# The router's noise in one tile, multiplied in PSUM, and its ranks summed in PSUM, in a retention and mixture-of-experts kernel

## The chip, the core and the metric

The kernel runs on one core of a Trainium2 chip. A core has five engines that run at the same time, each with its own queue of instructions, executed in order: TensorE (PE in the profile; its weight loads are PEld), VectorE (DVE), ScalarE (ACT), GpSimd (POOL) and SyncE (SP), which here only issues DMAs. GpSimd and ScalarE can issue DMAs too. SBUF is the large on-chip memory of 128 partitions; PSUM is the smaller one that TensorE writes its results to, and that VectorE and ScalarE can read and write. The metric is the device time of one execution in microseconds. A profile is one separately profiled execution; its span runs from the first to the last instruction.

## What is computed

Two layers run one after the other. The first is a retention layer, attention without a softmax, in which each score is multiplied by a power of a decay that depends on the head:

```python
scores = scale * np.matmul(q, k.transpose(0, 1, 3, 2))          # 8 batches, 8 heads, 576 tokens, 64 wide
gamma = 1.0 - 2.0 ** (-5.0 - np.arange(H, dtype=np.float32))
Dmat = np.where(rel >= 0, gamma[:, None, None] ** rel[None, :, :], 0.0)
attn = np.matmul(scores * Dmat[None], v)
```

Its output, 4608 tokens of 512 numbers, goes through a mixture of 8 experts. A router picks two experts for each token:

```python
logits = x @ w_gate
noise_scale = np.log1p(np.exp(x @ w_noise))
noisy_logits = logits + noise_scale * noise          # noise: 4608 x 8, an input
top2 = np.argpartition(-noisy_logits, 2, axis=1)[:, :2]
top2_w = softmax over the two chosen values
out[token] = sum over its two experts e of  top2_w * (relu(x[token] @ w1[e]) @ w2[e])
```

## The kernel before, in words

**Order.** The engines' order is the order in which the program is written: the whole of attention and routing, and then the expert stage, stand under a manual schedule, so no scheduler moves anything. A tile framework adds the waits between engines.

**Attention.** Sixteen units (four pairs of batches, two groups of four heads, two batches of the pair) go through a software pipeline, one unit a step `n`. For a unit, SyncE loads q, k and v four units ahead (lines 170 and 175; the last 64 tokens of each batch, the tail, at 182). GpSimd multiplies k and q by the decay and casts them to bf16 (`cast_k`, line 203, and `cast_q`, line 212), ScalarE casts v (189). TensorE transposes (253), forms the scores (268), which VectorE masks into SBUF (273), then the states (292) and the outputs (318 and 326). Tails have their own scores (343, masked at 345) and outputs (356 and 359). The input tiles hold four units at a time.

**Routing.** When the four units of a pair of batches and its tail are done, `route(bp)` starts; it is a generator, and the main loop runs one of its pieces between the parts of each later step (`piece()`), so that its instructions stand in the queues among those of attention. It runs four times. A pair has 1152 tokens, held as 9 columns of 128: columns 0 to 3 and 4 to 7 are four tokens a partition of the first and the second batch, column 8 holds the two tails, 64 partitions each. One PSUM bank, `R`, is kept for the router: it takes the logits (line 518), the ranks (614 to 622), the sums of the columns (columns 200 to 215 of the bank), the lists of tokens (288 to 367), and holds two constants (368 to 376, and from 384 on).

In a route, VectorE adds the two halves of the logits into `lg` (525 and 526); ScalarE computes log(1 + exp) of the noise half (529 and 530) into the SBUF tile `nl`; VectorE multiplies by the noise, eight columns from `noise` and the ninth from `noiset` (553 and 554), and adds the gate's logits (555). Two searches for the largest value follow (`first_max`, lines 545 to 550), and a one-hot matrix `M` of the two choices (572). From `M`, TensorE counts how many earlier tokens chose each expert (614 to 622), in PSUM as `pr`. VectorE adds the counts of earlier pairs (`base`, line 627, into the SBUF tile `prf`), adds the two choices of each token (629, into `prs`), multiplies both by `M` (630 and 631, into the third and fourth part of `pd`), and sums over experts (633). It then brings `base` up to date (636; in two routes 638 too), copies a transposed row of tokens out of PSUM (512) and works out positions (643 to 663). GpSimd computes what the rows carry beside the token (584 to 608, 635, 652 to 656), and SyncE stores them (658). Two comparisons make one-hot matrices (670 to 677), from which TensorE makes the lists of tokens of each expert (687).

**What is queued around it.** GpSimd's casts for a later unit stand in its queue behind its routing instructions, SyncE's later loads behind the route's stores. The noise is loaded once, in step 1, by SyncE (`load_noise`, lines 480 and 484), behind the gate's weights (1191 and 1192) and ahead of unit 6's q, k and v.

**Experts.** Five tiles of 256 tokens run early, among the last steps of attention (`early`, lines 365 to 440); the other 35 follow, each with a gather by GpSimd (848), transposes (957), two matmuls (973 and 993), and the sum of a token's two experts (1034, scattered at 1040).

Of the kernel before, what the change touches and what calls it, by code (L numbers as in the profile page):

```python
# [10 lines left out]
F32 = mybir.dt.float32  # L11
BF16 = mybir.dt.bfloat16
I32 = mybir.dt.int32
AX = mybir.AxisListType.X
Alu = mybir.AluOpType
Act = mybir.ActivationFunctionType

P = 128
N = 4608
NCOL = N // P  # L20
E = 8
# [23 lines left out]
HD = 64  # L45
MID = 288
NC9 = 9
# [85 lines left out]
class Attention:  # L133
# [3 lines left out]
    def __init__(self, tc, ctx, raw, K, q, k, v):  # L137
        self.tc, self.nc, self.K = tc, tc.nc, K
        self.src = dict(q=q, k=k, v=v)
        nc = self.nc  # L140
        ep = lambda n, b, **kw: ctx.enter_context(tc.tile_pool(name=n, bufs=b, **kw))
        self.cp = ep("at_c", 1)
        self.raw = raw
        self.bf = ep("at_bf", 2)
        self.tp = ep("at_t", 2)
        self.sp = ep("at_s", 2)
        self.xp = ep("at_x", 2)
        self.ps = ep("at_ps", 1, space=bass.MemoryType.PSUM)
        self.Tb = [self.cp.tile([P, 2, 4, P], BF16, name=f"Tb{j}") for j in range(4)]
        self.u = {}  # L150
        self.tails = {}
        self.T = {}
        self.xT = {}
# [289 lines left out]
class Router:  # L443
    def __init__(self, tc, ctx, K, at, wgn, moe_noise, xd, keep):
        self.tc, self.nc, self.K, self.at = tc, tc.nc, K, at
        self.wgn, self.xd, self.keep = wgn, xd, keep
        nc = self.nc
        self.sp = ctx.enter_context(tc.tile_pool(name="rt", bufs=2))
        self.one = ctx.enter_context(tc.tile_pool(name="rt1", bufs=1))
        self.rows = ctx.enter_context(tc.tile_pool(name="rtx", bufs=3))  # L450
        self.noise = self.one.tile([P, 8, 4, E], F32, name="noise")
        self.noiset = self.one.tile([P, 4, E], F32, name="noiset")
        self.L = self.one.tile([P, NH], F32, name="L")
        self.moe_noise = moe_noise
        self.w = self.one.tile([P, 2, NCOL], F32, name="w_all")
        self.ov = self.one.tile([P, 2, NCOL], F32, name="ov_all")

        bank = self.bank = at.ps.tile([P, 512], F32, name="R", bufs=1)
        self.iota = bank[:, 384:]
        self.local = bank[:, 368:368 + NC9]  # L460

        self.base = self.one.tile([P, 2, E], F32, name="base")
        self.atleast = {}
# [13 lines left out]

    def load_noise(self, q):
        nm = self.moe_noise.rearrange("(b s) e -> b s e", b=8)
        q.dma_start(out=self.noise.rearrange("p b r e -> p b (r e)"),  # L480
                    in_=nm[:, :512, :].rearrange("b (p r) e -> p b (r e)", r=4))
        nt = nm[:, 512:, :].rearrange("(p b) s e -> s b p e", b=2)
        for j in range(2):
            q.dma_start(out=self.noiset[j * HD:(j + 1) * HD], in_=nt[:, j])

    def route(self, bp):

        nc, K, sp = self.nc, self.K, self.sp
        V = nc.vector
        ps = self.at.ps  # L490
        C = NC9
# [32 lines left out]
        lg = sp.tile([P, C, 2 * E], F32, name="lg")  # L524
# [2 lines left out]
        yield  # L527
        nl = sp.tile([P, C, E], F32, name="nl")
        nc.scalar.activation(nl, lg[:, :, E:], Act.Exp)
        nc.scalar.activation(nl, nl, Act.Ln, bias=1.0)  # L530
        yield
        row(2)
        yield
# [1 line left out]
        def col(name):  # L535
            return sp.tile([P, C], F32, name=name)
# [13 lines left out]
            V.tensor_reduce(w, s, AX, Alu.max)  # L550
            return m, w

        V.tensor_mul(nl[:, :8], nl[:, :8], self.noise[:, 2 * bp:2 * bp + 2].rearrange("p b c e -> p (b c) e"))
        V.tensor_mul(nl[:, 8], nl[:, 8], self.noiset[:, bp])
        V.tensor_add(nl, nl, lg[:, :, :E])
        yield
        m1, w1 = first_max(nl, "a")
        yield
# [11 lines left out]
        SH = [P, C, 2, E]  # L570
        M = sp.tile(SH, BF16, name="M")
# [10 lines left out]
        pd = sp.tile([P, 4] + SH[1:], F32, name="pd", bufs=1)  # L582
# [8 lines left out]
        r = col("r")  # L591
# [20 lines left out]
        pr = self.bank[:, :C * 2 * E].rearrange("p (c a e) -> p c a e", c=C, a=2)  # L612
# [10 lines left out]
                             stop=(c == C - 1), skip_group_check=True)  # L623
        yield

        prf = sp.tile(SH, F32, name="prf", bufs=1)
        V.tensor_tensor(prf, pr, self.base.unsqueeze(1).to_broadcast(SH), Alu.add)
        prs = sp.tile([P, C, E], F32, name="prs", bufs=1)
        V.tensor_tensor(prs, prf[:, :, 0], prf[:, :, 1], Alu.add)
        V.tensor_mul(pd[:, 2], M, prf)  # L630
        V.tensor_tensor(pd[:, 3], M, prs.unsqueeze(2).to_broadcast(SH), Alu.mult)
        yield
        V.tensor_reduce(red, pd, AX, Alu.add)
# [657 lines left out]
```

## Time and profile before

| | |
|---|---|
| median of 7 runs | 526.05 us (522.96 to 534.98) |
| the profiled execution | 526.33 us |
| its span | 524.3 us |
| its mean granted TensorE clock | 0.92 |
| busy PE, DVE, ACT, POOL | 426.5, 239.2, 275.3, 277.0 us |
| TensorE in 90 to 120 us | 23.5 of 30 us busy, granted clock 0.74 |
| TensorE in 210 to 300 us | 86.0 of 90 us busy, granted clock 1.00 |
| routes, from L525 to the last L677 | 56, 97, 135 and 171 us; to 86, 126, 160 and 190 us |

The profiled execution took 2.0 us more than its span. The page cuts the span into 40 slices of 13.1 us and gives each engine's busy share in tenths. In a timeline a row is: start, duration (both us), engine, line of the kernel, operation, output and inputs by the program's names with partitions x elements and type, and in brackets how long the engine had been idle before it and what released it. A PSUM tile of the router is called R, whichever part of the bank is meant. A line of the waits gives the total, the number and the longest. "DMA share" is the busy share of the core's 16 DMA engines; small pieces can take it slightly over 1.

### The profile page before, as it was taken

How to read it: one execution, taken by the hardware profiler on the slowest of the kernel's cores; microseconds unless marked ns; L12 is line 12 of the kernel's file. 1: busy time of each engine (PE TensorE's matmuls, PEld its weight loads, DVE VectorE, ACT ScalarE, POOL GpSimd, SP SyncE). 2: the span in 40 equal slices, each digit the busy share in tenths (PEclk: the TensorE clock that was granted, in tenths of full speed). 3: DMA queues.
4: the chain of work that ended last, by engine and by line, in shares of the span. 5: the costliest groups of instructions: out<-in, count | busy, mean ns of one | idle time of the engine just before them, and what ended most of it. 6: DMA issues, size and time to landing. Idle time of an engine off the chain costs nothing.

```text
span 524.3 us, 11762 instructions
## 1 busy us (share of the span) xinstructions
PE 426.5 (81%) x4688; PEld 298.7 (57%) x4688; DVE 239.2 (46%) x603; ACT 275.3 (53%) x405; POOL 277.0 (53%) x369
## 2 busy tenths in 40 slices
PE   1666766867878998999969988988988968989960
PEld 1555655656655775766636655654655636546630
DVE  2533688588693673432413522332442423334440
ACT  5677956866964865566517535434544514433200
POOL 8646457349762148724570571572465666466440
PEclk9979877776897999999999998997999999889995
DMA  8998999939947155677676576675559676343430
GB/s 248 273 266 183 277 258 299 301 60 246 234 77 180 43 205 181 229 241 251 199 220 210 168 241 219 209 216 198 183 192 309 214 236 228 125 138 128 139 121 2
DMA packets 92856, 104.18 MB, mean 199 GB/s; under 512 B 22135, under 2 KB 69752, under 8 KB 92800
## 3 DMA queue, kind: packets, MB, share of 16 engines
q1 hardware_dynamic: 78096, 70.07, 45.2%
q0 software_dynamic: 14176, 32.83, 21.7%
q8 instruction: 37, 0.61, 0.5%
q10 hardware_dynamic: 528, 0.52, 0.3%
q14 instruction: 19, 0.16, 0.1%
HBM read 84.66 MB, written 28.72 MB: 216 GB/s over the span
## 4 chain that ended last, share of the span: by engine, by line
PE 32%; issue 17%; POOL 10%; another core or an unknown queue 4%; DVE 3%; ACT 3%; DMA 2%; POOLq 0%; ACTq 0%; DVEq 0%
PE p L973 12%; PE po L993 10%; POOL prv L1002 4%; POOL xg L848 3%; POOL out_dram L1040 3%; PE x L413 3%; PE pt L957 2%; PE S L403 2%; PE T L403 1%; DVE hT L980 1%; DMA prv<-yd,ix 1%; DMA out_dram<-o,ix 1%; DMA raw_q<-xd,xi 1%; PE T L292 0%
## 5 line engine op out<-in xcount | busy, mean ns | idle before, releaser
L973 PE MATMUL p<-xgT,w 128*128 128x256 bf16 x1120 | 217.7, 276 | 16.7 <-issue 13.0
L993 PE MATMUL po<-w,hT 128*128 128x512 bf16 x560 | 213.4, 386 | 6.6 <-issue 6.3
L973 PEld LDWEIGHTS <-w 128*128 128x128 bf16 x1120 | 110.3, 99 | 99.0 <-issue 33.3
L980 DVE TENSOR_SCALAR hT<-p 128x512 bf16<-128x512 f32 x70 | 48.4, 691 | 189.1 <-PE p L973 102.5
L978 ACT ACTIVATE hT<-p 128x512 bf16<-128x512 f32 x70 | 41.8, 597 | 154.3 <-PE p L973 58.2
L1040 POOL DMA_INDIRECT out_dram<-o,ix x45 | 45.6, 1013 | 98.6 <-DVE o L1034 90.9
L848 POOL DMA_INDIRECT xg<-xd,xi x68 | 68.9, 1013 | 20.2 <-issue 17.7
L993 PEld LDWEIGHTS <-hT 128*128 128x128 bf16 x560 | 55.4, 99 | 16.4 <-issue 8.6
L1002 POOL DMA_INDIRECT prv<-yd,ix x45 | 45.1, 1002 | 25.2 <-issue 13.0
L273 DVE TENSOR_TENSOR S<-S,mask 128x1024 bf16<-128x1024 f32 x32 | 39.1, 1222 | 36.5 <-PE S L268 36.4
L922 ACT ACTIVATE w<-wst 128x1024 bf16<-128x1024 f32 x48 | 50.6, 1055 | 0.0
L203 POOL TENSOR_TENSOR kn<-raw_k,kg 128x1024 bf16<-128x1024 f32 x14 | 26.6, 1900 | 20.9 <-DMA raw_k<-in_k_dram 13.4
L960 ACT ACTIVATE xgT<-pt 128x1024 bf16<-128x1024 bf16 x35 | 35.7, 1019 | 1.4 <-ACT raw_v L416 0.7
L1034 DVE SCALAR_TENSOR_TENSOR o<-po,g,prv 128x512 f32<-128x512 f32 x45 | 31.6, 742 | 0.8 <-PE po L993 0.8
L212 POOL TENSOR_TENSOR qb<-raw_q,qg 128x1024 bf16<-128x1024 f32 x15 | 28.5, 1903 | 0.0
L957 PE MATMUL pt<-ident,xg 128*128 128x128 bf16 x272 | 21.4, 220 | 2.1 <-ACT xgT L960 1.2
L268 PE MATMUL S<-QT,KT 64*64 64x128 bf16 x512 | 16.7, 260 | 7.4 <-DVE S L273 4.0
L332 ACT ACTIVATE xT<-x 128x512 bf16<-128x512 f32 x32 | 17.3, 592 | 9.5 <-PE x L326 9.4
L255 ACT ACTIVATE QT<-tr 128x1024 bf16<-128x1024 bf16 x16 | 16.4, 1022 | 10.9 <-PE tr L253 10.9
L292 PE MATMUL T<-vn,kn 64*64 64x64 bf16 (+2 forms) x512 | 21.7, 223 | 0.0
L253 PE MATMUL tr<-ident,qb 128*128 128x128 bf16 x128 | 12.9, 260 | 10.7 <-POOL Tb L1174 9.3
L298 ACT ACTIVATE Tb<-T 64x512 bf16<-64x512 f32 x32 | 18.8, 587 | 4.1 <-PE tr L394 2.8
(211 smaller groups left out, 592.1 us busy)
## 6 DMA issues: line engine op xcount, KB each, us to landing
wst<-in_moe_w_dram SPq DMA_DIRECT2D x48, 512.0 KB
raw_k<-in_k_dram SPq DMA_DIRECT2D x32, 256.0 KB
raw_v<-in_v_dram SPq DMA_DIRECT2D x32, 256.0 KB
yd<-y SPq DMA_DIRECT2D x16, 512.0 KB
raw_q<-in_q_dram SPq DMA_DIRECT2D x15, 512.0 KB
xd<-xr SPq DMA_DIRECT2D x12, 396.0 KB
w<-in_moe_w_dram POOLq DMA_DIRECT2D x4, 1024.0 KB
yd<-raw_v SPq DMA_DIRECT2D x5, 512.0 KB
```

What stands on the lines that cost most here:

```text
L273: nc.vector.tensor_tensor(S.rearrange("p h c r t -> p (h c) (r t)"), p.rearrange("p h (c r) t -> p (h c) (r t)", r=2), self.K["mask"].rear ...
L848: tc.nc.gpsimd.indirect_dma_start(out=xg[:, s, :], out_offset=None, in_=xd[:, :], in_offset=IOff(ap=keep["xi"][:, j:j + 1], axis=0), bound ...
L922: nc.scalar.activation(W[e][:, k * F:(k + 1) * F], t, Act.Copy)
L957: nc.tensor.transpose(pt[:, di, s * P:(s + 1) * P], xb[:, di * P:(di + 1) * P], K["ident"])
L960: return lambda: nc.scalar.activation(xgT, pt, Act.Copy)
L973: nc.tensor.matmul(p1[:, f2, :], lhsT=w[:, o:o + P], rhs=xgT[:, di, :], start=(di == 0), stop=(di == KD - 1))
L978: nc.scalar.activation(hT[:, 2 * fp:2 * fp + 2, :], p1, Act.Relu)
L980: V.tensor_relu(hT[:, 2 * fp:2 * fp + 2, :], p1)
L993: nc.tensor.matmul(po[s], lhsT=hT[:, fi, s * P:(s + 1) * P], rhs=w[:, o:o + DM], start=(fi == 0), stop=(fi == KF - 1))
L1002: nc.gpsimd.indirect_dma_start(out=prv[i % NP][:, s, :], out_offset=None, in_=yd[:rows, :], in_offset=IOff(ap=st[i]["ix"][:, s, 1:2], axis=0),
L1034: V.scalar_tensor_tensor(o[:, s, :], st[i]["po"][s], st[i]["g"][:, s:s + 1], prv[i % NP][:, s, :], Alu.mult, Alu.add)
L1040: ins = nc.gpsimd.indirect_dma_start(out=out[:, :], out_offset=IOff(ap=st[i]["ix"][:, s, 0:1], axis=0), in_=st[i]["o"][:, s, :], in_offset ...
```

## The change

The noise is laid out in one tile, for each pair of batches nine columns with the tail as the ninth. Its main part is loaded by two DMAs in place of one (one for each batch of a pair), the tails by two as before, into the ninth column. ScalarE writes its logarithm into the bank R (columns 0 to 71, where the logits were) and not into SBUF; one multiplication over nine columns, in place in PSUM, takes the place of two in SBUF, and the addition reads the product from PSUM. The counts with `base` added stay in PSUM, in place; the sum over the two choices is a reduction from PSUM to PSUM (columns 216 to 287), and the two products with `M` read PSUM. The tiles `prf`, `prs` and `noiset` are gone. On the engines, VectorE has one instruction fewer in each route, SyncE one DMA more in all; the order is otherwise the same. In the lists of waits, the multiplication of the first route waits for four noise loads and for ScalarE, and the first product (line 630) now waits for the reduction before it.

```diff
-        self.noise = self.one.tile([P, 8, 4, E], F32, name="noise")
-        self.noiset = self.one.tile([P, 4, E], F32, name="noiset")
+        self.noise = self.one.tile([P, 4, NC9, E], F32, name="noise")
...
     def load_noise(self, q):
         nm = self.moe_noise.rearrange("(b s) e -> b s e", b=8)
-        q.dma_start(out=self.noise.rearrange("p b r e -> p b (r e)"),
-                    in_=nm[:, :512, :].rearrange("b (p r) e -> p b (r e)", r=4))
+        nb = nm[:, :512, :].rearrange("(x b) (p r) e -> b p x (r e)", b=2, r=4)
+        for b in range(2):
+            q.dma_start(out=self.noise[:, :, 4 * b:4 * b + 4].rearrange("p x r e -> p x (r e)"), in_=nb[b])
         nt = nm[:, 512:, :].rearrange("(p b) s e -> s b p e", b=2)
         for j in range(2):
-            q.dma_start(out=self.noiset[j * HD:(j + 1) * HD], in_=nt[:, j])
+            q.dma_start(out=self.noise[j * HD:(j + 1) * HD, :, 8], in_=nt[:, j])
...
         nl = sp.tile([P, C, E], F32, name="nl")
         nc.scalar.activation(nl, lg[:, :, E:], Act.Exp)
-        nc.scalar.activation(nl, nl, Act.Ln, bias=1.0)
+        sg = self.bank[:, :C * E].rearrange("p (c e) -> p c e", c=C)
+        nc.scalar.activation(sg, nl, Act.Ln, bias=1.0)
...
-        V.tensor_mul(nl[:, :8], nl[:, :8], self.noise[:, 2 * bp:2 * bp + 2].rearrange("p b c e -> p (b c) e"))
-        V.tensor_mul(nl[:, 8], nl[:, 8], self.noiset[:, bp])
-        V.tensor_add(nl, nl, lg[:, :, :E])
+        V.tensor_mul(sg, sg, self.noise[:, bp])
+        V.tensor_add(nl, sg, lg[:, :, :E])
...
-        prf = sp.tile(SH, F32, name="prf", bufs=1)
-        V.tensor_tensor(prf, pr, self.base.unsqueeze(1).to_broadcast(SH), Alu.add)
-        prs = sp.tile([P, C, E], F32, name="prs", bufs=1)
-        V.tensor_tensor(prs, prf[:, :, 0], prf[:, :, 1], Alu.add)
-        V.tensor_mul(pd[:, 2], M, prf)
+        V.tensor_tensor(pr, pr, self.base.unsqueeze(1).to_broadcast(SH), Alu.add)
+        prs = self.bank[:, 216:216 + C * E].rearrange("p (c e) -> p c e", c=C)
+        V.tensor_reduce(prs, pr.rearrange("p c a e -> p c e a"), AX, Alu.add)
+        V.tensor_mul(pd[:, 2], M, pr)
         V.tensor_tensor(pd[:, 3], M, prs.unsqueeze(2).to_broadcast(SH), Alu.mult)
```

## The prediction

> **What bounds the kernel now.** I read the page's slices first, then the waits after 60 us, then the timelines of VectorE, GpSimd, TensorE and SyncE around the routing, and last the chain that ended last. The page says that there are two kernels in one span: up to about 190 us no engine is full, afterwards TensorE is.
>
> ```profile
> PE   1666766867878998999969988988988968989960
> DVE  2533688588693673432413522332442423334440
> POOL 8646457349762148724570571572465666466440
> DMA  8998999939947155677676576675559676343430
> ```
>
> A slice is 13.1 us. The change touches only the routing, four times between 57 and 190 us. Its worth is therefore what the attention stage loses to routing, passed on to the expert stage, where TensorE is busy 86 of 90 us (210 to 300) and nothing absorbs a later or earlier start. The chain that ended last is recorded from 138.65 us on only; from there it runs without a gap through attention, VectorE (olo and oh at 152.8 to 160) and the early expert tiles.
>
> Now the instructions that the change rewrites, on the timelines (start us, us, engine, line): VectorE, GpSimd, then TensorE.
>
> ```profile
> 59.45 1.35 DVE L553 TENSOR_TENSOR nl<-nl,noise 128x64 f32<-128x64 f32 x1
> 60.73 1.88 DVE L554 TENSOR_TENSOR nl<-nl,noiset 128x8 f32<-128x8 f32 x1
> ...
> 70.61 1.71 DVE L629 TENSOR_TENSOR prs<-prf 128x72 f32<-128x72 f32 x1
> 72.24 2.01 DVE L630 TENSOR_TENSOR pd<-M,prf 128x144 f32<-128x144 bf16 x1
> ...
> 109.65 2.03 DVE L630 TENSOR_TENSOR pd<-M,prf 128x144 f32<-128x144 bf16 x1
> 111.60 2.00 DVE L631 TENSOR_TENSOR pd<-M,prs 128x144 f32<-128x144 bf16 x1
> ...
> 118.34 1.35 DVE L670 TENSOR_TENSOR olo<-R,lo 128x1152 f16<-128x1152 f32 x1
> ```
>
> ```profile
> 58.83 1.90 POOL L203 TENSOR_TENSOR kn<-raw_k,kg 128x1024 bf16<-128x1024 f32 x1 [4.26 <-DMA raw_k<-in_k_dram]
> 60.69 1.90 POOL L212 TENSOR_TENSOR qb<-raw_q,qg 128x1024 bf16<-128x1024 f32 x1
> ...
> 118.05 1.89 POOL L203 TENSOR_TENSOR kn<-raw_k,kg 128x1024 bf16<-128x1024 f32 x1
> ```
>
> ```profile
> 74.86 0.60 PE L356 MATMUL x<-St,vt 128*64 128x128 bf16 x2 [2.23 <-DVE St L345]
> ...
> 113.99 0.59 PE L356 MATMUL x<-St,vt 128*64 128x128 bf16 x2 [3.03 <-DVE St L345]
> ```
>
> Multiplying 8 elements takes 1.88 us at 60.73 and 0.16 us in the third route at 137.91. The slow ones end where a GpSimd cast ends: L553 at 60.80 (kn ends 60.73), L554 at 62.61 (qb ends 62.59). All have both inputs in SBUF. L670, one input of which is in the PSUM bank R, takes 1.35 us under the cast at 118.05 and the same 1.35 us at 152.72 with GpSimd free. So the losses are waits for GpSimd's casts, and a PSUM operand is free of them. Against their lowest rows (0.22, 0.16, 0.23, 0.30, 0.30 us) the five lines lose 9.6 us over four routes: 2.8 at 59 us, 3.2 at 70 us, 3.4 at 109 us, nearly nothing in routes three and four, when GpSimd casts nothing.
>
> **The change part by part.** *First route, multiplication.* New order: multiply, add, both with a PSUM operand, then L545 (reduce), L547, L548. From 59.45 at 0.27 us a step, L547 starts at 60.26. It has both inputs in SBUF, as has L548: the stall is inherited. L547 gets through when kn ends (60.73), L548 when qb ends (62.59), L550 starts at 62.67 instead of 63.78. Gain 1.1 us, not 2.8. It reaches the path: from 58.3 to 68.8 VectorE has no idle time, and TensorE waits 2.42 us for L512 at 67.83.
>
> *First route, ranks.* From 70.28: base add, reduce, two products at 0.33, 0.35, 0.22, 0.22 us; L345 can start at 71.4 instead of 74.39, and its scores are in PSUM by 71.24. TensorE is then late itself: L292 runs until 72.63, so of L356's lateness only the wait of 2.23 us goes. What follows hangs on TensorE's transposes (L507), by when qb is over. Gain 2.2 us. GpSimd's next casts follow VectorE (idle 1.79 and 1.80 us for L636 and L660), so they move too.
>
> *Second route, ranks.* L345 could start at 110.3; TensorE's 3.03 us go. But L638 (base with atleast, both in SBUF; not in the first route) arrives at 111.8, with qb at work until 113.44. It ends at 113.7 in place of 115.2; from L512 (115.74) to the next mask (117.21) are 1.47 us, so the mask starts at 115.2. Gain 2.0 us. This route's multiplication meets no cast.
>
> [...]
>
> *PSUM operands.* Five instructions a route get a PSUM source that they had not. [...] An instruction that reads and writes PSUM is in no row; between 0 (L627 reading, L467 writing 128 elements in 284 ns, both normal) and a doubled time per element (72, 144 and 144 elements at the 1.02 ns between L545 and L633: 0.4 us a route, 1.1 us in all). I take 0. The Ln on ScalarE now writes PSUM: its row is 0.26 us, bounds 0.2 to 0.35; in the first route it ended 0.5 us before its reader, in the others VectorE waits 0.4 us for it.
>
> *Instructions.* One multiplication fewer (-0.07 us a route, as it overlapped). The reduce reads 144 elements for 72: from L545 (72, 230 ns) and L633 (576, 742 ns) it costs 0.30 against 0.23 us. The product L630 now waits for the reduce, +0.12. Net +0.1 us in each route; with its stalls counted above, one 0.1 remains for the third, whose VectorE is on the chain at 150.7 us.
>
> *One DMA more on SyncE.* At 37.7 us the noise is sent in two halves.
>
> ```profile
> 37.72 0.83 SPq L480 DMA_DIRECT2D noise<-in_moe_noise_dram  x1
> 38.59 2.18 SPq L484 DMA_DIRECT2D noiset<-in_moe_noise_dram  x2
> 40.87 0.55 SPq L170 DMA_DIRECT2D raw_q<-in_q_dram  x1
> ```
>
> Behind it queue unit 6's loads, the tails and unit 7. There this is dear: DMA share is 0.38 from 40 to 44 us, because SyncE has been issuing small transfers, and afterwards ScalarE waits 3.19 us for raw_v (51.20) and GpSimd 4.26 us for raw_k (58.83). Issuing 512 pieces of raw_q takes 0.55 us, the noise's 1024 take 0.83, so two halves cost 1.1 and the delay is 0.3 us; the bounds are 0 (absorbed) and 1.5 (the longer L484). I take 0.3: the same pieces are sent. The routes move with it. The multiplication now waits for all four noise loads, in place by about 45 us and needed at 59.
>
> Sum: -1.1 - 2.2 - 2.0 + 0.1 + 0.3 = -4.9 us. The profiled execution took 526.33 us, a span of 524.3 and 2.0 around it; it becomes 521.4, a span of 519.4. The median of the seven is 0.28 lower and gives 521.15; I say 521.2.
>
> **The rivals.**
>
> *Every stall goes* (no heir): 9.6 - 0.4 us, 517. For it: PSUM operands run free. Against: L547, L548 and L638 stand next with two SBUF inputs, and L292 on TensorE.
>
> *Half of it is absorbed.* TensorE's granted clock is 0.81, 0.74 and 0.83 in the windows 60 to 90, 90 to 120 and 120 to 150; if work packed closer is granted less, or ScalarE's queue (Exp behind a table load until 66.05) holds the next transposes, 1 to 3 us remain: 524.
>
> *The loads bound the stage, and it gets slower.* From 56 to 107 us the DMA share is 1.0 to 1.15 almost throughout. If attention ran at the pace of its loads, the route's stalls would be slack, and only the extra DMA would count, at 37 us where supply is the bound: 0.3 to 1.5 us, and 0.1 to 2 us for PSUM: 527.5. It decides once unit 11's raw_k, issued until 83.8, lands after the cast needs it (92.95 now, 89.6 then). Against: after 58.83 no engine waits for a load, and GpSimd's waits are for VectorE and TensorE. A fall by 3% of the clock in the last 224 us (0.95 and 0.92, TensorE busy 186) would also cost over 5 us; no row ties it to the change.
>
> *It doesn't do what it says*: if an instruction with a PSUM operand still waits, only the extras remain, about +0.5 us; L670's two equal rows speak against it.
>
> **How the numbers follow.** The worked case 0.50, own range 519.5 to 523 (reduce rule, PSUM and SyncE bounds); every stall 0.12; half absorbed 0.20; loads or clock, or no effect, 0.18, a third of it beyond 531 us. The runs before spread from 522.96 to 534.98 around 526.05, so about 1% (5.3 us) is what a measurement can tell from no change, and the worked case ends just inside it. Faster by over 1%: 0.12 and about half of 0.50, 0.38; slower by over 1%: a third of 0.18 and a share for causes not in the list, 0.11; within: 0.51. Range 517 to 528.
>
> **What would show it.** Right: the multiplication at 59 us takes under 0.3 us, L547 and L548 (numbered one higher then) take 0.5 to 1.9; the products at 70 and 109 us take 0.3; L356 follows L292 without a wait; L638 takes up to 1.9 at about 108; the first expert transposes begin 5 us earlier. Wrong: these rows are as said and TensorE waits for something else just as long, or GpSimd waits longer for raw_k at 58.8.

## The result, and the profile after

The changed kernel takes 521.7 us (median of 26 runs, 516.68 to 530.5), the kernel before 527.18 us in the same comparison (63 runs, 520.6 to 538.07). The ratio is 0.9915, with a 95% interval of 0.9891 to 0.9939: 4.5 us less, where the prediction said 4.9 us (a ratio of 0.9907). A ratio compares only those runs of each kernel that lie within 1.5% of its fastest; a difference of means, given with ±, takes all runs. The profiled execution took 521.16 us, with a span of 519.1, against 526.33 and 524.3. The mean granted TensorE clock is 0.92 in both profiles.

First, two rows of the page's slices, to be laid beside those of the kernel before. Nothing of the shape has changed: TensorE's slices are mostly at 6 to 8 tenths up to about 170 us, and mostly at 8 or 9 afterwards.

```profile
PE   1666776868778998999969988997988996979960
DVE  2533696695792763433323512341443442433440
```

The timeline of VectorE in the first and the second route (start us, us, engine, line, operation, output and inputs) holds nearly all that the change did. R is the PSUM bank. Rows in between are left out at each "...".

```profile
59.67 0.24 DVE L554 TENSOR_TENSOR R<-R,noise 128x72 f32<-128x72 f32 x1
59.95 0.23 DVE L555 TENSOR_TENSOR nl<-R,lg 128x72 f32<-128x72 f32 x1
60.22 0.23 DVE L546 TENSOR_REDUCE am<-nl 128x9 f32<-128x72 f32 x1
60.48 1.87 DVE L548 TENSOR_TENSOR scr<-nl,am 128x72 f32<-128x72 f32 x1
...
69.31 0.30 DVE L626 TENSOR_TENSOR R<-R,base 128x144 f32<-128x144 f32 x1
69.65 0.32 DVE L628 TENSOR_REDUCE R<-R 128x72 f32<-128x144 f32 x1
70.00 0.30 DVE L629 TENSOR_TENSOR pd<-M,R 128x144 f32<-128x144 bf16 x1
70.22 0.30 DVE L630 TENSOR_TENSOR pd<-M,R 128x144 f32<-128x144 bf16 x1
...
71.10 0.74 DVE L632 TENSOR_REDUCE red<-pd 128x72 f32<-128x576 f32 x1
...
72.56 1.02 DVE L642 CAST rki<-red 128x9 int32<-128x9 f32 x1
...
108.82 1.62 DVE L637 TENSOR_TENSOR base<-base,atleast 128x16 f32<-128x16 f32 x1
```

GpSimd's casts in the same stretches (in brackets the idle time before, and what ended it):

```profile
58.49 1.91 POOL L203 TENSOR_TENSOR kn<-raw_k,kg 128x1024 bf16<-128x1024 f32 x1 [3.67 <-PE S L268]
60.36 1.90 POOL L212 TENSOR_TENSOR qb<-raw_q,qg 128x1024 bf16<-128x1024 f32 x1
...
69.80 1.90 POOL L203 TENSOR_TENSOR kn<-raw_k,kg 128x1024 bf16<-128x1024 f32 x1
71.66 1.90 POOL L212 TENSOR_TENSOR qb<-raw_q,qg 128x1024 bf16<-128x1024 f32 x1
...
108.51 1.91 POOL L212 TENSOR_TENSOR qb<-raw_q,qg 128x1024 bf16<-128x1024 f32 x1
```

The multiplication took 1.35 and 1.88 us in two instructions and takes 0.24 in one. The addition and the reduce behind it run beside the cast at 0.23 us. The sum over the two choices and the first product, 1.71 and 2.01 us before, are a reduce of 0.32 and a product of 0.30. None of them waits, though a cast runs beside L554, L555 and L546, and from 69.80 us (kn) beside the end of the reduce and both products. A PSUM operand costs little either, in the medians of the four routes: L554, in place over 72 elements, takes 236 ns, where L553 took 224 to 226 for 64 of SBUF without a stall; L626, in place, takes 306 ns, where L627 wrote the same sum to SBUF in 298; the reduce takes 316 ns, which the prediction had at 0.30 us. The stall itself is still there. At 60.48 us L548, the next instruction with two SBUF inputs, takes 1.87 us and ends at 62.35, where the cast of qb ends (62.26). At 108.82 us the maximum with atleast takes 1.62 us and ends (110.44) with the cast of qb in that route (110.42). And L642, a cast with a single input in SBUF that takes 0.16 us elsewhere, takes 1.02 us at 72.56 and ends where qb ends.

TensorE's state products, which waited 2.23 and 3.03 us for L345, wait for nothing (no bracket):

```profile
71.06 0.39 PE L356 MATMUL x<-St,vt 128*64 128x128 bf16 x2
...
107.92 0.40 PE L356 MATMUL x<-St,vt 128*64 128x128 bf16 x2
```

On SyncE's queue the noise takes 1.78 us for 0.83, its tails 1.27 us for 2.18, and raw_q of unit 6 starts at 41.05 us instead of 40.87:

```profile
37.85 1.78 SPq L481 DMA_DIRECT2D noise<-in_moe_noise_dram  x2
39.68 1.27 SPq L484 DMA_DIRECT2D noise<-in_moe_noise_dram  x2
41.05 0.55 SPq L170 DMA_DIRECT2D raw_q<-in_q_dram  x1
```

To see where the time went, the mask multiplications of the scores (L273) serve as milestones, since VectorE reaches each of them after the work in question. Seven are used: a and b begin at 58.31 and 66.23 us in the kernel before, with the first route's noise and first choices between them; c at 78.08, behind the first route's ranks; d and e at 108.01 and 117.21, on the two sides of the second route's ranks; f and g at 128.49 and 155.74, with most of the third route between them. In microseconds:

| stretch | before | after | difference |
|---|---|---|---|
| a to b, multiplication | 7.92 | 6.74 | -1.18 |
| b to c, ranks | 11.85 | 9.37 | -2.48 |
| c to d | 29.93 | 30.50 | +0.57 |
| d to e, ranks | 9.20 | 6.78 | -2.42 |
| f to g, third route | 27.25 | 29.60 | +2.35 |
| first expert transposes begin | 206.53 | 202.91 | -3.62 |

The three places of the prediction gain 6.1 us in this pair of profiles; 2.9 us of it are gone again by g. The first expert transposes begin 3.6 us earlier, where the prediction had 5, and the span is shorter by 5.2, so that the last 1.6 us of this pair come from the expert stage, in which nothing was changed. The experiments have to say three things: whether the first row is the multiplication's doing, whether the ranks carry the gain, and whether the losses of rows three and five belong to the change.

### The profile page after: what moved, and what is told of

It reads as the page before. It is cut to its first block, busy times and chain, and to the rows that moved or that the text cites. A ratio compares the mean times of both kernels' runs of the same rounds, so it can differ in the third digit from the quotient of the medians.

```text
span 519.1 us, 11762 instructions
## 1 busy us (share of the span) xinstructions
PE 424.1 (82%) x4688; PEld 297.1 (57%) x4688; DVE 234.1 (45%) x599; ACT 275.4 (53%) x405; POOL 277.4 (53%) x369
## 4 chain that ended last, share of the span: by engine, by line
PE 59%; DVE 7%; issue 7%; ACT 5%; another core or an unknown queue 1%; DMA 1%; POOL 0%; ACTq 0%; POOLq 0%; DVEq 0%
PE p L972 24%; PE po L992 22%; PE x L413 3%; PE pt L956 3%; DVE S L273 2%; PE S L403 2%; PE T L403 2%; DVE olo L669 1%; DVE o L1033 1%; ACT xr L510 1%; DVE oh L676 1%; DVE oh L673 1%; PE R L686 1%; PE tr L507 1%
## 5 line engine op out<-in xcount | busy, mean ns | idle before, releaser
L972 PE MATMUL p<-xgT,w 128*128 128x256 bf16 x1120 | 217.8, 277 | 14.0 <-issue 9.2
L992 PE MATMUL po<-w,hT 128*128 128x512 bf16 x560 | 213.4, 385 | 7.3 <-issue 5.5
L972 PEld LDWEIGHTS <-w 128*128 128x128 bf16 x1120 | 110.3, 99 | 95.9 <-issue 29.7
L992 PEld LDWEIGHTS <-hT 128*128 128x128 bf16 x560 | 55.4, 99 | 17.9 <-issue 10.0
L273 DVE TENSOR_TENSOR S<-S,mask 128x1024 bf16<-128x1024 f32 x32 | 39.1, 1221 | 37.6 <-PE S L268 37.3
L1019 ACT ACTIVATE y<-po,g 128x512 f32<-128x512 f32 x24 | 16.2, 688 | 10.9 <-PE p L972 3.7
```

Of the source, the lines that this page charges most:

```text
L273: nc.vector.tensor_tensor(S.rearrange("p h c r t -> p (h c) (r t)"), p.rearrange("p h (c r) t -> p (h c) (r t)", r=2), self.K["mask"].rear ...
L972: nc.tensor.matmul(p1[:, f2, :], lhsT=w[:, o:o + P], rhs=xgT[:, di, :], start=(di == 0), stop=(di == KD - 1))
L992: nc.tensor.matmul(po[s], lhsT=hT[:, fi, s * P:(s + 1) * P], rhs=w[:, o:o + DM], start=(fi == 0), stop=(fi == KF - 1))
```

## The experiments

The kernel before took 526, 487 and 535 us in the three comparisons, so times are held only against the kernel before of the same one. "±" is two standard errors of the difference of means.

### One half at a time

Theory: the ranks in PSUM give most of the gain, the multiplication about 1 us. Rival: it is the layout with one multiplication fewer, or the place of the loads. Three kernels take the change apart. Ranks alone:

```diff
-        V.tensor_mul(sg, sg, self.noise[:, bp])
-        V.tensor_add(nl, sg, lg[:, :, :E])
+        V.tensor_mul(nl[:, :8], nl[:, :8], self.noise[:, 2 * bp:2 * bp + 2].rearrange("p b c e -> p (b c) e"))
+        V.tensor_mul(nl[:, 8], nl[:, 8], self.noiset[:, bp])
+        V.tensor_add(nl, nl, lg[:, :, :E])
```

(with the noise's tiles, loads and the Ln as before the change)

> The ranks stay in PSUM, the noise is loaded and multiplied as in the kernel before. Port theory (two SBUF inputs wait for a GpSimd cast, a PSUM operand does not): L553 and L554 stall again at 59 us (1.3 and 1.9 us), the products at 70 and 109 us do not; 2.2 + 2.0 - 0.1 us gained, ratio to before 0.992 (0.990 to 0.995). If the gain of the change came from the noise alone: 1.00. If the routes' stalls were slack: 1.00.

The noise alone (layout and multiplication in PSUM):

```diff
-        V.tensor_tensor(pr, pr, self.base.unsqueeze(1).to_broadcast(SH), Alu.add)
-        prs = self.bank[:, 216:216 + C * E].rearrange("p (c e) -> p c e", c=C)
-        V.tensor_reduce(prs, pr.rearrange("p c a e -> p c e a"), AX, Alu.add)
-        V.tensor_mul(pd[:, 2], M, pr)
+        prf = sp.tile(SH, F32, name="prf", bufs=1)
+        V.tensor_tensor(prf, pr, self.base.unsqueeze(1).to_broadcast(SH), Alu.add)
+        prs = sp.tile([P, C, E], F32, name="prs", bufs=1)
+        V.tensor_tensor(prs, prf[:, :, 0], prf[:, :, 1], Alu.add)
+        V.tensor_mul(pd[:, 2], M, prf)
```

> The noise in one tile and multiplied in PSUM, the ranks in SBUF as before. Port theory with heirs: L548 inherits the stall at 60.5 us, 1.1 us gained there and 0.1 to 0.3 lost to the extra DMA: ratio 0.9985 (0.997 to 1.001); the products at 70 and 109 us stall for 1.5 to 2 us again. Without heirs: 2.5 us gained, 0.995.

The layout alone: the noise's one tile and one multiplication, but in SBUF; the ranks as before.

```diff
-        V.tensor_mul(sg, sg, self.noise[:, bp])
-        V.tensor_add(nl, sg, lg[:, :, :E])
+        V.tensor_mul(nl, nl, self.noise[:, bp])
+        V.tensor_add(nl, nl, lg[:, :, :E])
```

> One tile of noise and one multiplication over nine columns, but in SBUF; the logarithm goes to SBUF, the ranks stay in SBUF. Port theory: the multiplication stalls until the first cast ends (about 1.3 us) and the addition behind it, two SBUF inputs too, until the second (about 1.9 us), so nothing but 0.1 us of one instruction is gained and the extra DMA costs 0.1 to 0.3: ratio 1.000 (0.998 to 1.002). If fewer and larger instructions were the gain: below 0.998.

Medians against 526.3 us of the kernel before (35 runs; 12 of each other): ranks alone 522.71 (means differ by -2.9 ± 1.7 us), noise alone 525.86 (-0.7 ± 1.5), layout alone 526.73 (+0.1 ± 1.9). The ratios (1.0001, 1.0059 and 1.0065, each about ± 0.005) show no gain for any of them: the shortest run of the kernel before, 517.91 us, stands 4.2 us below the next, and leaves only the 13 shortest of its 35 runs in the ratio. So against the kernel before this comparison alone is unclear. Beside each other, 12 runs against 12, the ranks alone stand 3.0 ± 2.2 us below the layout alone. The ranks carry a gain, and the layout none that can be measured. Of the noise half this comparison can't say whether it is 0 or 2 us.

The layout alone shows the stall going to an heir in its plainest form. The timelines of VectorE and GpSimd in that kernel:

```profile
60.45 0.42 DVE L553 TENSOR_TENSOR nl<-nl,noise 128x72 f32<-128x72 f32 x1
60.90 1.83 DVE L554 TENSOR_TENSOR nl<-nl,lg 128x72 f32<-128x72 f32 x1
```

```profile
60.74 1.90 POOL L212 TENSOR_TENSOR qb<-raw_q,qg 128x1024 bf16<-128x1024 f32 x1
```

The one multiplication arrives 0.3 us before the first cast ends (60.78), and the addition, which did not stall in the kernel before (0.23 us), takes 1.83 us and ends with the cast of qb (62.73 and 62.64). The expectations name their theory after a port; no trace shows one. What the rows show is that VectorE's instruction ends with GpSimd's cast.

### The two halves once more, with the whole change beside them

> The changed kernel once more, for the comparison with the other three on one chip. Theory: 0.99 of the time before (5 us less), and at least 2 us below the kernel that has only the ranks in PSUM if the multiplication in PSUM is worth the 1.1 us that the prediction gives it and passes them on; if the noise half is worth nothing by itself, the two are within 1 us of each other.

> Noise as before the change, ranks in PSUM. By the prediction's sum (2.2 and 2.0 us) 4.2 us less than before, 0.992. If the noise half is worth 1.1 us, it stands 1 us above the whole change; if its gain is a matter of where GpSimd's cast happens to stand when the multiplication comes, it is level with the whole change, within 1 us.

The whole change took 483.02 us, the ranks alone 485.23, the kernel before 487.28: ratios 0.9915 (0.9889 to 0.994) and 0.995 (0.9929 to 0.997). In means: -4.4 ± 1.3 and -2.6 ± 0.9 us. The ranks alone were expected to give 4.2 us. The whole change stands 1.8 ± 1.4 us below the ranks alone, so the noise half is worth something there. The noise half alone, run in a third comparison, could not sharpen this: 533.59 us against 535.15, -1.8 ± 4.9.

> The noise half alone (layout, multiplication in PSUM), ranks as before the change. If it is worth what the last comparison of the whole change with the ranks alone gives (2.2 us), it stands 2 us below before, 0.9955; if by itself it is lost again further on, as the first look at it said (525.9 against 526.3 us), it is level with before.

What it is worth as far as mask b is read from the traces, and more sharply than from the times. VectorE with the ranks alone (second profile):

```profile
59.70 0.99 DVE L553 TENSOR_TENSOR nl<-nl,noise 128x64 f32<-128x64 f32 x1
60.61 1.88 DVE L554 TENSOR_TENSOR nl<-nl,noiset 128x8 f32<-128x8 f32 x1
62.53 0.23 DVE L555 TENSOR_TENSOR nl<-nl,lg 128x72 f32<-128x72 f32 x1
```

In each kernel the last stalled instruction ends with the cast of qb, 0.02 to 0.09 us after it in the rows of GpSimd (for the noise alone in those of the first profile). What counts is how much of the routing is still to do from that moment until mask b. From the end of the stalled instruction to the start of b:

| kernel | stalled instruction that ends with qb | mask b | left to do |
|---|---|---|---|
| before | second multiplication, 62.61 | 66.23 | 3.62 |
| ranks alone, two profiles | second multiplication, 63.08 and 62.49 | 66.70 and 66.11 | 3.62 and 3.62 |
| layout alone | addition, 62.73 | 66.09 | 3.36 |
| noise alone, two profiles | comparison L548, 63.25 and 62.53 | 66.08 and 65.36 | 2.83 and 2.83 |
| whole change, two profiles | comparison L548, 62.35 and 63.17 | 65.17 and 65.99 | 2.82 and 2.82 |

The noise half gains 0.80 us by mask b: three instructions (addition, reduce, comparison) of 0.27 us a step are over when qb ends. The rest of the 1.18 us in the first pair of profiles is phase: how long after mask a the stall ends (4.30 us in the profile of before, 3.92 in that of after; 3.26 and 3.93 in the two of the ranks alone). The layout by itself gives one step of 0.26. How much of the 0.80 us reaches the end is not shown: the first expert transposes begin at 202.91 and 203.05 us in the two profiles of the whole change, and at 202.79 and 203.16 in the two of the ranks alone.

### The heirs

If a stall is handed on, an edit that also takes the heirs out of its way moves it once more. In this kernel the noisy logits, the flags and the first choice's index lie in the bank, and base is raised by atleast there:

```diff
-        V.tensor_add(nl, sg, lg[:, :, :E])
+        rg = lambda o, n: self.bank[:, o:o + n * C].rearrange("p (c e) -> p c e", c=C)
+        nl = rg(72, E)
+        V.tensor_add(nl, sg, lg[:, :, :E])
...
-            s = sp.tile([P, C, E], F32, name="scr", bufs=1)
+            s = rg(144, E)
...
-            w = col(name + "w")
+            w = self.bank[:, 216:216 + C] if name == "a" else col(name + "w")
...
-        nl2 = sp.tile([P, C, E], F32, name="nl2", bufs=1)
+        nl2 = rg(0, E)
...
-        V.tensor_add(self.base, self.base, pn)
-        if bp + 1 in self.atleast:
-            V.tensor_tensor(self.base, self.base, self.atleast[bp + 1], Alu.max)
+        if bp + 1 in self.atleast:
+            V.tensor_add(pn, self.base, pn)
+            V.tensor_tensor(self.base, pn, self.atleast[bp + 1], Alu.max)
+        else:
+            V.tensor_add(self.base, self.base, pn)
```

(low1 is computed earlier, so that VectorE is done with the bank before TensorE writes the ranks)

> On top of the changed kernel the noisy logits, the row-maximum flags and the first choice's index lie in PSUM too, and base is raised by atleast in PSUM: the two heirs of the stall (the comparison at 60.5 us, 1.87 us, and the maximum with atleast at 108.8 us, 1.62 us) lose their second SBUF input. Theory (a stall is handed on to the next instruction that uses the shared port): both rows fall to about 0.23 and 0.16 us, but at 60 us TensorE is busy without a gap until the scores at 64.7 us, so the mask comes at most 0.5 us earlier, and at 109 us the cast of the rank (1.02 us at 72.6 us already) takes the rest of the stall, so 0.3 us remain there: 0 to 1 us less than the changed kernel. Rival (the two stalls are on the path): 1.6 + 1.5, 3 us less.

> The kernel with the heirs in PSUM once more, one look for its rows: 0.24 us for the comparison, and the cast of the rank inherits at 108 us with 0.9 to 1.1 us. 4 to 6 us less than before.

483.03 us in the comparison where the whole change took 483.02; in means 0.8 ± 1.6 us below it, which cannot be told from nothing. (The second run, 526.08 us against 523.56 to 544.26, serves for its rows alone.) VectorE's timeline of the first:

```profile
62.02 0.24 DVE L548 TENSOR_TENSOR R<-R,am 128x72 f32<-128x72 f32 x1
...
67.98 0.17 DVE L594 TENSOR_SCALAR r<-d 128x9 f32<-128x9 f32 x1 [1.31 <-ACT d L583]
...
107.84 0.17 DVE L639 TENSOR_TENSOR base<-R,atleast 128x16 f32<-128x16 f32 x1
...
108.44 1.01 DVE L646 CAST rki<-red 128x9 int32<-128x9 f32 x1
```

Both stalls are gone from their rows, and the theory's next heir has the second one: the cast of the rank takes 1.01 us (1.02 in the second profile). From d to e 0.42 us are gained (6.36 for 6.78), where 0.3 were expected. In the first route mask b comes 1.67 us sooner after a (5.06 for 6.73), more than expected, but c does not follow: from a to c it is 15.23 us against 15.59, 0.36 us less. Taking 1.6 us out of VectorE there is worth a quarter of it, because ScalarE comes next: at 67.98 us VectorE waits 1.31 us for the exponential of L583 (1.28 in the second profile). In the profile of after, ScalarE works without a gap from 56.86 us to the same exponential (L579, at 66.98), and a table load of 1.28 us at 65.69 stands right ahead of it. From b to c the kernel takes 10.17 us for 8.86, just these 1.31 us more. The profile of the whole change has a wait of 0.43 us at the same place, its second profile and those of the kernel before and the ranks alone none. The rival, 3 us, falls.

### What VectorE waits for

All of this assumes that VectorE waits for the end of a whole GpSimd instruction. Each of the two casts is issued as two halves:

```diff
-        eng.tensor_tensor(kn.rearrange("p r c h d -> p (c h) r d"),
-                          d.pop("rawk").rearrange("p c h (r d) -> p (c h) r d", r=2),
-                          self.kg[:, hq].rearrange("p c h r -> p (c h) r").unsqueeze(3).to_broadcast(
-                              [P, 8, 2, HD]), Alu.mult)
+        rk = d.pop("rawk")
+        for c in range(2):
+            eng.tensor_tensor(kn[:, :, c].rearrange("p r h d -> p h r d"),
+                              rk[:, c].rearrange("p h (r d) -> p h r d", r=2),
+                              self.kg[:, hq, c].unsqueeze(3).to_broadcast([P, 4, 2, HD]), Alu.mult)
```

(and the cast of qb in the same way)

> The changed kernel with each of GpSimd's two casts of a unit issued as two of half the size (about 1.04 us each by the row of 512 elements). If VectorE waits for the end of a whole GpSimd instruction, the comparison at 60.5 us no longer takes 1.87 us: it ends with the half that is under way (at most 1.0 us) and the next instruction with two SBUF inputs waits for the next half. If the two share the port cycle by cycle, the row stays at 1.8 us or above. In time: no gain, 0 to 2 us more, since GpSimd's pairs get 0.3 us longer and the stall only goes to two instructions in turn.

> The changed kernel with GpSimd's casts in halves, now timed. The comparison at 60.5 us and its successor take 0.8 to 0.9 us each, as one look showed. If the sum of a stall stays (1.2 us of loss instead of 1.6), it is level with the changed kernel, 0.991 of before; if halving sets VectorE free earlier at each route and unit, 1 to 2 us less, 0.988.

VectorE and GpSimd in the first profile of this kernel (two halves of a cast stand in one row, x2; L550 and L551 are the comparison and its successor):

```profile
60.66 0.79 DVE L550 TENSOR_TENSOR scr<-nl,am 128x72 f32<-128x72 f32 x1
61.56 0.90 DVE L551 TENSOR_TENSOR scr<-scr,desc 128x72 f32<-128x72 f32 x1
```

```profile
58.32 2.04 POOL L205 TENSOR_TENSOR kn<-raw_k,kg 128x512 bf16<-128x512 f32 x2 [3.02 <-DMA raw_k<-in_k_dram]
60.32 2.04 POOL L216 TENSOR_TENSOR qb<-raw_q,qg 128x512 bf16<-128x512 f32 x2
```

The comparison no longer takes 1.87 us: it ends in the middle of qb, at 61.45, and the next instruction with two SBUF inputs ends with qb's second half, at 62.46 (the halves end at about 61.34 and at 62.36). In the second profile the two rows take 0.53 and 0.89 us, and their ends (61.76 and 62.75) are 0.99 us apart, about the 1.02 us of a half. So in these rows VectorE's instruction is held until GpSimd's ends, and the two do not share within an instruction. In time the halves give nothing that can be told: 481.9 us in a single run beside 483.02, and in six runs 529.58 against 535.15 of the kernel before (-5.9 ± 4.3 us, which includes the whole change's 4.4).

### The loads

The rival of a slower kernel had the extra DMA at 37 us as its root. Here the noise is loaded behind unit 6's loads instead of ahead of them:

```diff
+            if n == 2:
+                rt.load_noise(nc.sync)
             if n % 4 == 2 and n // 4 < 3:
...
-                rt.load_noise(nc.sync)
```

> The changed kernel with the four noise loads moved in SyncE's queue from ahead of unit 6's loads to behind them, ahead of the tails. If the transfers of small pieces in front of unit 6 hold up the stage: unit 6's k arrives about 3 us earlier (GpSimd's wait of 3.42 us before it shrinks to under 1), up to 1.5 us gained on the changed kernel, ratio to before 0.989. If tails and unit 7, which are not moved, set the pace: equal to the changed kernel, 0.9915 (0.990 to 0.993).

523.83 us against 526.3 of the kernel before: -2.7 ± 1.6 us, no better than the ranks alone in the same comparison (-2.9); its ratio, 1.0009 ± 0.005, is as unclear as theirs, and the changed kernel itself was not in this comparison. Unit 6 no longer waits for its keys, but the next unit waits longer for its own; GpSimd's timeline:

```profile
59.35 1.90 POOL L203 TENSOR_TENSOR kn<-raw_k,kg 128x1024 bf16<-128x1024 f32 x1 [6.34 <-DMA raw_k<-in_k_dram]
```

6.34 us here, 4.26 before, and the cast begins 0.5 us later than before. (In the first profile of the changed kernel unit 6 waits 3.42 us for its keys; in both, the next unit's cast is held by TensorE, 3.67 and 4.24 us, and begins at 58.49 and 59.32.) The order of the loads on SyncE moved the wait from one unit to the next.

### Where 2.9 us went back

The stretches of all profiles, with the granted clock from f to g. The stalls of the ranks (d to e) part the kernels in two groups: 9.2 us with the ranks in SBUF, 6.4 to 6.8 in PSUM.

| kernel | a to c | c to d | d to e | f to g | clock f to g |
|---|---|---|---|---|---|
| before | 19.77 | 29.93 | 9.20 | 27.25 | 0.92 |
| layout alone | 18.53 | 28.85 | 9.20 | 29.03 | 0.79 |
| noise alone | 18.30 | 28.22 | 9.16 | 28.66 | 0.88 |
| noise alone, again | 18.05 | 28.83 | 9.20 | 28.61 | 0.87 |
| after | 16.11 | 30.50 | 6.78 | 29.60 | 0.78 |
| after, again | 15.59 | 30.17 | 6.78 | 28.55 | 0.80 |
| ranks alone | 15.74 | 28.84 | 6.79 | 30.05 | 0.78 |
| ranks alone, again | 16.41 | 30.49 | 6.79 | 28.88 | 0.83 |
| noise behind unit 6 | 17.00 | 30.50 | 6.79 | 29.84 | 0.79 |
| heirs | 15.23 | 28.76 | 6.36 | 28.91 | 0.83 |
| heirs, again | 15.20 | 28.79 | 6.36 | 30.40 | 0.78 |
| halves | 15.49 | 28.74 | 6.66 | 28.88 | 0.84 |
| halves, again | 16.01 | 30.49 | 6.64 | 30.08 | 0.78 |

From f to g the profile of before is the shortest of thirteen, and has the highest clock. The layout alone, which has all the stalls of the ranks, takes 29.03 us at a clock of 0.79. TensorE's 524 matmuls of this stretch are busy for 22.07 us in the profile of before and for 24.47 in that of after, and this 2.4 us is the whole difference. So 2.35 us is in the main the difference of two executions, and not the price of the change. There may be a price all the same: in the mean of the groups the kernels with the ranks in PSUM take 29.5 us for 28.4 from f to g, at a clock of 0.80 for 0.87, and 29.7 for 29.0 from c to d. That is 1.8 us of about 6 given back, which would bring the sum of the places near the measured 4.4. The ranks alone say the same: their two places gain about 5.3 us, and the time 2.6 ± 0.9. Four profiles against nine, some 1.5 us apart within a group, are not enough to call the clock's part in it shown. No kernel was made that holds the clock still.

## Why the prediction was right

Its time, 521.2 us, is 0.5 us below the measured 521.7, its -4.9 us stand against -4.5, and the result lies within 1% as held likeliest. By its steps:

- **PSUM operands don't stall: right.** 0.23 to 0.32 us for all of the new form; only the base addition (69.31) met no cast in these rows. The price of a PSUM operand, taken as 0 between bounds of 0 and 1.1 us, is near 0: the base addition, which reads and writes 144 elements in PSUM, takes 306 ns against 298 for L627, which read them there and wrote to SBUF; the product L629, with one operand in PSUM, takes 303 against 297 for L630 of the kernel before, unstalled and all in SBUF. No run shows the up to 2 us that the rival of the loads adds for PSUM; the rows show these 6 to 8 ns an instruction.
- **A reduce doesn't wait, as the steps of the first route have it: right.** No run of the kernel before shows the reduce rule that the range counts with: there no cast ran beside L545 (62.91 us) or L633 (75.06 and 114.19). In the profile of after L546 took 0.23 us at 60.22 beside the end of kn's cast and the beginning of qb's, and the reduce L632 0.74 us at 71.10 beside the same two; without a cast beside them the two took 0.23 and 0.73 to 0.75 us in the kernel before.
- **First route, multiplication, -1.1: the mechanism held, the size is 0.80.** The step that failed is "L547 gets through when kn ends, L548 when qb ends": two heirs, one for each cast. The first of them (L548 after the change) came 0.08 us after kn had ended (60.40), so it alone took the whole of qb's stall, and one instruction fewer was over when qb ended. The profiled pair's 1.18 looks like the prediction, but 0.4 of it is phase.
- **Ranks, -2.2 and -2.0: mechanism right, sizes low.** 2.48 and 2.42 us in the profiled pair. The second route had its predicted heir, the maximum with atleast, which ended with the cast as said, and the products, L345 and the scores behind it moved up. The first route had an heir that the prediction did not see, the rank's cast L642 (1.02 us), and gained as much as said in spite of it. Between the executions the stretch b to c is 11.75 to 11.85 us with the stalls; with the ranks in PSUM it is 9.37 in the profile of after (0.43 of it VectorE's wait for ScalarE), 8.86 in the second profile of it and in both of the ranks alone, and 9.62 with the noise behind unit 6.
- **One DMA more, +0.3: right in size, partly by luck.** The next load starts 0.18 us later, and mask a 0.12 us. The two halves of the noise took 1.78 us, not the 1.1 of the working; the tails behind them took 0.91 us less than before, which the working did not have.
- **The sum.** The places gained 5.7 to 6.1 us (0.8 + 2.5 to 2.9 + 2.4), where the prediction had 5.3; the times moved by 4.4 and 4.5. So the number is nearer than its terms, and that is in part luck: gains larger than said, and something given back that the sum did not hold. Nor did it pass on whole to the expert stage, as the prediction assumed: the first expert transposes begin at 203.0 us in the mean of the two profiles of the whole change, and at 206.4 in that of the four profiles with the ranks in SBUF, 3.4 us and not 5. The prediction's rival "half of it is absorbed" named the granted clock and ScalarE's queue as the ways. The table above leans to the clock and does not settle it; the wait for ScalarE's exponential is in the rows, 0.43 us in one of the two profiles of the whole change.
- **The other rivals.** Every stall goes: no, three heirs stand in the trace, and freeing two of them in the heirs kernel moved the time by -0.8 ± 1.6 us. The loads bound the stage: no, VectorE's gain arrives at e, and shifting the noise's loads moved waits from unit to unit. It doesn't do what it says: no, by every row.

## What to carry to other kernels

When an engine's instruction is slow because it waits for another engine's instruction to end, count what will be done by that end, and not the length of the slow row: here 3.2 us of slow rows were worth 0.8 us, three instructions of 0.27 us that came to stand ahead of the wait. Look for the next instruction of the same kind behind the one that is freed, single-input casts too (1.02 us for 0.16 here), and cost the edit up to there. Then ask which engine's turn comes next: with the first route's heir freed, the wait for ScalarE took back 1.31 of 1.67 us. And before a stretch's difference in one pair of profiles is put down to an edit, look at it in kernels that lack the edit: phase moved 0.4 us here, and 2.35 us stood between two profiles with granted clocks of 0.92 and 0.78.

## What was not expected of the hardware

A cast of nine elements from SBUF (128x9, f32 to int32) waits for GpSimd like an instruction with two SBUF inputs: 1.02 and 0.90 us in the two profiles of the whole change (72.56 and 72.99 us), 1.03 and 1.01 in the first of the heirs kernel (73.31 and 108.44), instead of 0.16, each time until qb ended. With GpSimd's casts in halves, a tensor_scalar on 2 x 9 integers took 0.90 us (at 72.62 in the first profile) instead of 0.18.

The medians of these kernels are 522 to 535 us in three comparisons and 482 to 487 in one. Nearly all of that lies in the expert stage: from its first transposes to the end 314 to 323 us, against 278 to 280. In the profile of after, TensorE sat idle there ahead of L972 and L992 with no cause shown (the two "issue" rows, total us, times, longest); the group of the same matmul in the second profile of it has no idle time at all.

```profile
PE p L972 <- issue: 9.2, 19, 0.9
PE po L992 <- issue: 5.5, 11, 0.8
```

```profile
L972 PE MATMUL p<-xgT,w 128*128 128x256 bf16 x1120 | 213.0, 275 | 0.0
```

These two rows are 14.7 of the 36.5 us between the two profiles in this stage; TensorE is also busy 13.7 us longer with about as many matmuls (276.8 us for 1970 of them from 200 us to 4.7 us before the end, 263.0 for 1975 in the other), at granted clocks of 1.00, 0.95 and 0.91 in the stretches 200 to 300, 300 to 400 and from 400 us on, against 0.98, 1.00 and 0.94. What decides between the two is open; the ratio of after to before is 0.9915 under both.
